# Strassen on a second level in the down products of an attention + SwiGLU kernel

## The chip, the cores and the metric

One core of a Trainium2 chip runs the whole kernel in one launch, in fp32. The metric is the device time of one execution in microseconds (us).

## What is computed

Cut to what matters, the reference is

```python
# transnormer attention: batch 8, heads 8, seq 576, head_dim 64
kv  = einsum('bhsd,bhse->bhde', k, v)          # 64x64 per head, over the sequence
o   = einsum('bhsd,bhde->bhse', q, kv)
x   = o / sqrt(mean(o*o, -1) + 1e-6) * g_norm  # -> (4608, 512): tokens x model
# SwiGLU: d_model 512, d_ff 1536
h   = silu(x @ w_gate) * (x @ w_val)           # the "up" stage
out = h @ w_out                                # the "down" stage, 4608 x 512
```

## The kernel before

The 4608 tokens are cut into 9 blocks of 512. The blocks run one after the other, and each has an **up** stage (gate and value products and their SwiGLU, class `Up` or `Inner`) and a **down** stage (class `Down`). Both stages save multiplications with Winograd's form of Strassen's algorithm: a product of 2x2 blocks is done by 7 products of blocks and some sums, with weight combinations made once and kept. The seven products are numbered 1 to 7 in the code, and `CHAIN` says which PSUM tile each adds to: 1, 6, 7, 4 run into one bank of tile `b`, 2 has tile `a`, 5 and 3 share one bank of tile `c`. PSUM has three buffers of `b`, two of `c`, one of `a` and two of `m`. A product that continues a bank must wait until the sum so far was read out of it.

From block 2 on (`DEEP = 2`) the up stage is Strassen on two levels: each of the outer 7 products is itself done by 7 products of 128x128 blocks (`Inner`). The weight blocks that this needs and that aren't kept in SBUF are prepared once, in block 1, and parked in DRAM. `Stream` loads them back in each later block, 51 DMAs of up to 256 KB, through a ring of nine `t` tiles. `Stream.pump` issues a load as soon as, in program order, the tile nine places back has been released.

The down stage of the kernel before is Strassen on one level. `Down.multiply` issues for each of its 7 products 12 matmuls of a 128x128 stationary block with 256 moving columns. Products 1, 6, 7 and 4 are copied out of PSUM by ScalarE (`after1`, `after6`, `after7`, `after4`), the others are added by VectorE. Three of the seven weight combinations are subtractions on GpSimd (`turn_t`), nine of them a block. VectorE makes the operand sums (`h_sums`, `turn_s3`, the one in `after2`).

While the down products run, the attention of the next block is done in between, by the closures of `Att.steps`: after product 1 `whole` (64 small matmuls, squares, root, scale, and the two 32x32 block transposes of `blocks_x`), after product 5 `place_x` (16 DMAs, 8 on the SP queue and 8 on ScalarE's, that put the transposed blocks of x in place), and after product 2 `end` (the gain on ScalarE, then the eight operand sums of x and xi on VectorE that the next up stage begins with).

The program is written down in that order, and a scheduler of the tile framework then moves instructions within it. What it leaves is a fixed order for each engine. The helper lambdas `add`, `sub` and `mul` are lines 111, 112 and 113, so most elementwise rows of the profile carry one of these three lines. `Inner`'s matmuls are line 728, `Quad`'s (so all of `Down`'s) line 565, the attention's lines 316 (k times v) and 361 (q times that).

Of the kernel before, what the change touches and what calls it, by code (L numbers as in the profile page):

```python
# [8 lines left out]
F32 = mybir.dt.float32  # L9
# [5 lines left out]
P = 128  # L15
# [3 lines left out]
def kernel(  # L19
# [41 lines left out]
    nc = tc.nc  # L61
# [4 lines left out]
    T = 4  # L66
    BLK = P * T
    HB = BLK // 2
    HD = DM // 2
# [3 lines left out]
    NP = NF // 2  # L73
# [12 lines left out]
    x_pool = pool("x", 1)  # L86
    h_pool = pool("h", 1)
    s_pool = pool("s", 1)
# [26 lines left out]
    def ring():  # L115

        return r_pool.tile([P, 4, BLK], F32, name="r")

    class Words:
# [12 lines left out]
        def __init__(self, src, shape):  # L132
            self.raw = ld_pool.tile([P, LD], U32, name="ld")[:, 0 : 2 * BLK]
            dst = self.raw.rearrange("p (a b) -> p a b", a=shape[0])
            self.sent = nc.sync.dma_start(out=dst, in_=src)
            self.shape = shape
            self.begun = False
# [55 lines left out]
    class Att:  # L193
# [308 lines left out]
        def steps(self):  # L502


            def whole():
                self.product(0, (m_psum, a_psum))
                self.product(1, (m_psum, b_psum))
                self.root(0, 2)
                for i in range(2):
                    self.scale(i)  # L510
                self.halves.append(self.scaled)
                self.blocks_x()

            def end():
                self.gain_x()
                self.sums()

            if self.n >= TURNED:
                return {1: whole, 5: self.place_x, 2: end}

            def last():
                self.turn_x(1)
                if self.n:
                    self.sums()

            def middle():
                self.turn_x(0)
                self.half(1, (m_psum, b_psum))


            return {1: lambda: self.half(0, (m_psum, a_psum)), 6: middle, 2: last}
# [128 lines left out]
    class Inner:  # L660
# [101 lines left out]
        def made3(self, p, e, q):  # L762
            if p != 4:
                return
            h = self.ffn.h[:, 4 * self.d : 4 * self.d + 4]
            c11, c12, c21, c22 = (self.whole(*i) for i in ((1, 1), (3, 1), (3, 0), (1, 0)))

            engine = nc.gpsimd if 4 * self.d + 4 < NF else nc.vector
            mul(engine, h[:, :, 0:HB], c11, c12)
            nc.scalar.activation(out=c21, in_=c21, func=ACT.Silu)  # L770
            mul(engine, h[:, :, HB:BLK], c21, c22)
            self.ffn.ended = self.ffn.h_sums(2 * self.d, 2, engine)


    RESIDENT = (1, 6, 2, 3)
# [8 lines left out]
        ((4, 5), (3, 5)), ((7, 4),), ((4, 2), (4, 3)), ((4, 7), (3, 7)), ((4, 4), (3, 4)),  # L784
    )

    class Stream:


        def __init__(self):  # L790
            self.dram = [dram.tile([P, len(LEAVES), 2, P], F32, name=f"w{d}") for d in range(NP // 2)]
            self.places = [sorted(map(LEAVES.index, ops)) for ops in CHUNKS]
            self.at = {LEAVES[i]: (c, m) for c, places in enumerate(self.places) for m, i in enumerate(places)}
            self.tiles, self.uses, self.next, self.held = {}, {}, [], []

        def enable(self, n):
            if DEEP <= n < NB:
                self.next += [(n, d, c) for d in range(NP // 2) for c in range(len(CHUNKS))]
                self.pump()

        def pump(self):

            while self.next and not self.held[-9]:
                n, d, c = key = self.next.pop(0)
                i, k = self.places[c][0], self.places[c][-1]
                count = len(CHUNKS[c])
                self.tiles[key] = t_tile(key).rearrange("p l (f c) -> p l f c", f=2)
                self.uses[key] = 2 * count
                nc.sync.dma_start(out=self.tiles[key][:, 0:count], in_=self.dram[d][:, i : k + 1 : max(k - i, 1)])

        def use(self, n, d, o, p, f):
            c, i = self.at[o, p]
            key = n, d, c
            self.uses[key] -= 1
            if not self.uses[key]:
                self.free(key)
            return self.tiles[key][:, i, f]

        def free(self, key):
            self.held = [None if k == key else k for k in self.held]  # L820
# [3 lines left out]
    def t_tile(key=None):  # L824

        stream.held.append(key)
        return t_pool.tile([P, 2, 2 * P], F32, name="t")
# [27 lines left out]
    class Down(Quad):  # L855
        def __init__(self, ffn):
            super().__init__(NP)
            self.ffn = ffn
            self.t = {}
            self.final = ffn.n == NB - 1  # L860
            if self.final:
                self.apart["c"] = None

        def turn_t(self, p, after=None):

            pairs = wo.rearrange("p (j e) d -> p e j d", e=2)
            of = {5: pairs[:, 1, :, HD:DM], 7: pairs[:, 0, :, 0:HD], 4: pairs[:, 1, :, 0:HD]}[p]
            self.t[p] = []
            for i in range(0, NP, 2):
                t = t_tile((self.ffn.n, p))  # L870
                turned = sub(nc.gpsimd, t, of[:, i : i + 2], pairs[:, 0, i : i + 2, HD:DM])
                if after:
                    tc.add_manual_dep(
                        turned.ins, after.ins.name,
                        mybir.DependencyInfo(mybir.DependencyClass.Sync, mybir.DependencyReason.DATA), reason="order",
                    )
                self.t[p] += [t[:, 0], t[:, 1]]

        def multiply(self, p):
            super().multiply(p)  # L880
            if p in self.t:
                stream.free((self.ffn.n, p))
            if p == 7:
                stream.enable(self.ffn.n + 1)
            stream.pump()

        def order(self, p):
            order = [(e, i) for e in range(2) for i in range(self.steps)]
# [45 lines left out]
        def add_c(self, o, u):  # L934
# [4 lines left out]
            for e, c in enumerate((self.ps["c"], self.apart["c"])):  # L939
                add(nc.vector, o[:, e], c[:, e], u[:, e])  # L940

    class Ffn:
        def __init__(self, n, att):
            self.n, self.att = n, att
# [9 lines left out]
        def h_sums(self, j, k, engine):  # L954
# [4 lines left out]
            add(engine, s1, a21, a22)  # L959
            return sub(engine, a21, s1, a11)  # L960

        def make(self, count):
            for _ in range(count):
                steps = self.making or self.later
                if steps:
                    steps.pop(0)()

        def up(self, fill):

            self.s1 = s_pool.tile([P, NP, HB], F32, name="s1")  # L970
            units = []
            for d in range(NP // 2):
                if self.n < DEEP:
                    units += [Up(self, 2 * d), Up(self, 2 * d + 1)]
                else:
                    shared = {}
                    units += [Inner(self, d, g, shared) for g in range(4)]
            units[0].prepare()
            last = None
            for i, this in enumerate(units):  # L980
                if i + 1 < len(units):
                    units[i + 1].prepare()
                for unit, p in this.sequence(last):
                    if unit:
                        unit.multiply(p)
                        self.make(4)
                last = this
                fill.get(12 * (i + 1) // len(units), lambda: None)()
            self.down_ = Down(self)
            self.down_.turn_t(5)  # L990
            for unit, p in last.sequence(None):
                if unit is None:
                    last.multiply(p)

        def down(self, nxt):

            down = self.down_
            fill = nxt.steps() if nxt else {}
            for p in (1, 6, 5, 7, 2, 4, 3) if 5 in fill else (1, 5, 6, 7, 2, 4, 3):
                if p == 1:  # L1000
                    down.turn_t(7, self.ended)
                if p == 6:
                    down.turn_t(4, nxt.halves[0] if nxt and nxt.n >= TURNED else None)

                with tc.issue_after(nxt.multiplied.ins) if self.n == 0 and p in (5, 6) else ExitStack():
                    down.multiply(p)
                self.make(12)
                if p in fill:
                    fill[p]()
                if p in (5, 7) and self.n == DEEP - 1:  # L1010

                    with tc.issue_after(nxt.scaled.ins), tc.issue_after(nxt.placed.ins):
                        room = self.leaf_room if p == 5 else ring().rearrange("p f (s c) -> p (f s) c", c=P)
                        for step in self.latest.pop(0)(room):
                            step()
                if p == 1:

                    with tc.issue_after(nxt.q_turned.ins) if self.n == 0 else ExitStack():
                        down.turn_s3()
# [152 lines left out]
```

## Time and profile before

| | us |
|---|---|
| median of 3 runs | 1023.45 |
| lowest and highest | 1023.36 and 1024.01 |
| span of the profiled execution, first to last instruction | 1021.4 |
| PE (TensorE matmul) busy in it | 1006.0 |
| DVE (VectorE) busy | 701.1 |
| POOL (GpSimd) busy | 369.0 |
| ACT (ScalarE) busy | 227.9 |

The profiled execution is listed with its span alone; the 2 us to the median of the runs lie before its first and after its last instruction. In the profile PE is the row of matmuls and PEld that of the weight loads which overlap them. An fp32 matmul leaves two PE records, so "x24" of a down product are its 12 matmuls. DVE is VectorE, ACT ScalarE, POOL GpSimd, SPq the queue of DMAs that SyncE issues. In a timeline line the columns are the start, the duration (of all merged instructions together), the engine, the line, the operation, the tiles, the count, and in brackets the idle time ahead of it with what ended it.

### The profile page before, as it was taken

The numbers are of one execution on the slowest core, as the hardware profiler recorded it, in microseconds if no ns is written. First come the engines' busy times: TensorE is split into PE (matmuls) and PEld (weight loads), VectorE is DVE, ScalarE is ACT, GpSimd is POOL, SyncE is SP. The second block draws the span as 40 slices with busy tenths as digits, with TensorE's granted clock in tenths as the row PEclk, the third lists the DMA queues.
The fourth block names the chain that finished last, engine by engine and source line by source line (L and its number), as shares of the span: only waits on it lengthen the run. The fifth ranks groups of instructions, "written<-read, shape, count | busy, mean of one in ns | idle before, by whom it ended". The sixth has DMA issues, their size and how long they took to land.

```text
span 1021.4 us, 21409 instructions
## 1 busy us (share of the span) xinstructions
PE 1006.0 (98%) x8522; PEld 897.1 (88%) x8522; DVE 701.1 (69%) x1169; ACT 227.9 (22%) x353; POOL 369.0 (36%) x280
## 2 busy tenths in 40 slices
PE   6999999999999999999999999999999999999998
PEld 4544688888999989998999899988998999989997
DVE  2999688998665946685558566665669466946661
ACT  2765112121211221121121211111121211221110
POOL 0000263534055503561246315630555045513670
PEclk9999999999999999999999999999999999999999
DMA  8689643767888377845686568636772766066601
GB/s 237 203 255 271 124 77 108 187 165 156 250 210 255 60 176 203 252 92 129 209 238 144 96 195 247 177 60 201 231 199 46 177 195 190 22 167 201 191 27 42
DMA packets 273845, 170.26 MB, mean 167 GB/s; under 512 B 150609, under 2 KB 241873, under 8 KB 273745
## 3 DMA queue, kind: packets, MB, share of 16 engines
q1 hardware_dynamic: 238800, 164.42, 59.3%
q10 hardware_dynamic: 34880, 4.46, 2.7%
q8 instruction: 68, 1.11, 0.4%
q14 instruction: 33, 0.26, 0.1%
q0 software_dynamic: 64, 0.00, 0.0%
HBM read 138.02 MB, written 22.41 MB: 157 GB/s over the span
## 4 chain that ended last, share of the span: by engine, by line
PE 90%; DVE 6%; DMA 2%; issue 1%; ACT 1%; SPq 0%; DVEq 0%; ACTq 0%
PE b L728 26%; PE b L565 19%; PE c L728 13%; PE c L565 10%; PE a L728 6%; PE a L565 5%; PE b L1032 4%; PE c L1032 4%; PE m L316 2%; PE m L361 1%; DVE r L112 1%; DVE xi L112 1%; DVE r L111 1%; DMA h<-in_v_dram 1%; DVE t L112 1%
## 5 line engine op out<-in xcount | busy, mean ns | idle before, releaser
L111 POOL TENSOR_TENSOR r<-r 128x256 f32<-128x256 f32 (+1 forms) x105 | 110.8, 1061 | 300.9 <-DVE r L111 272.2
L111 DVE TENSOR_TENSOR r<-b,r 128x512 f32<-128x512 f32 (+1 forms) x273 | 161.9, 606 | 65.5 <-PE b L728 60.1
L112 POOL TENSOR_TENSOR t<-wo 128x512 f32<-128x512 f32 x81 | 114.5, 1438 | 212.4 <-DVE wo L111 102.9
L111 DVE TENSOR_TENSOR r<-c,r 128x512 f32<-128x512 f32 (+1 forms) x179 | 108.5, 617 | 89.0 <-PE c L728 54.8
L728 PE MATMUL b<-x,t 128*128 128x128 f32 x1092 | 151.3, 276 | 0.0
L111 DVE TENSOR_TENSOR r<-a,r 128x512 f32<-128x512 f32 (+1 forms) x99 | 62.5, 631 | 113.4 <-PE a L565 70.7
L728 PEld LDWEIGHTS b<-x,t 128*128 128x128 f32 x1092 | 136.5, 192 | 0.8
L728 PE MATMUL c<-xi,t 128*128 128x128 f32 x840 | 112.4, 276 | 0.4 <-DVE xi L111 0.4
L113 POOL TENSOR_TENSOR h<-r 128x1024 f32<-128x1024 f32 (+1 forms) x40 | 82.3, 2072 | 76.9 <-DVE r L111 73.9
L728 PEld LDWEIGHTS c<-xi,t 128*128 128x128 f32 x840 | 102.9, 192 | 0.5 <-DVE xi L111 0.5
L565 PE MATMUL b<-wo,h 128*128 128x256 f32 x432 | 100.1, 383 | 0.1
L565 PE MATMUL b<-t,h 128*128 128x256 f32 x432 | 96.9, 381 | 0.0
L565 PEld LDWEIGHTS b<-t,h 128*128 128x128 f32 x432 | 81.6, 190 | 11.3 <-issue 0.2
L565 PEld LDWEIGHTS b<-wo,h 128*128 128x128 f32 x432 | 79.9, 190 | 13.1 <-DVE h L113 2.5
L742 ACT COPY r<-b 128x512 f32<-128x512 f32 x63 | 36.9, 585 | 211.6 <-PE b L728 211.6
L728 PE MATMUL b<-xi,t 128*128 128x128 f32 x588 | 79.8, 276 | 0.0
L728 PEld LDWEIGHTS b<-xi,t 128*128 128x128 f32 x588 | 72.4, 192 | 0.0
L728 PE MATMUL b<-x,wg 128*128 128x128 f32 x336 | 52.7, 279 | 0.2 <-DVE x L112 0.2
L728 PE MATMUL b<-x,wv 128*128 128x128 f32 x336 | 51.4, 276 | 0.0
L565 PE MATMUL a<-wo,h 128*128 128x256 f32 x216 | 48.3, 379 | 0.0
L565 PE MATMUL c<-t,s 128*128 128x256 f32 x216 | 48.1, 380 | 0.0
L565 PE MATMUL c<-wo,h 128*128 128x256 f32 x216 | 48.1, 379 | 0.0
(133 smaller groups left out, 1565.7 us busy)
## 6 DMA issues: line engine op xcount, KB each, us to landing
t<-w SPq DMA_DIRECT2D x336, 256.0 KB, 3.6
out_dram<-r SPq DMA_DIRECT2D x17, 512.0 KB, 3.1
ld<-in_k_dram SPq DMA_DIRECT2D x26, 288.0 KB, 5.2
ld<-in_v_dram SPq DMA_DIRECT2D x26, 288.0 KB, 5.9
ld<-in_moe_w_gate_dram SPq DMA_DIRECT2D x12, 512.0 KB, 4.8
ld<-in_moe_w_val_dram SPq DMA_DIRECT2D x12, 512.0 KB, 4.7
ld<-in_moe_w_out_dram SPq DMA_DIRECT2D x12, 512.0 KB, 4.9
w<-t SPq DMA_DIRECT2D x18, 256.0 KB, 3.0
```

The source lines that it names most:

```text
L111: add = lambda e, o, a, b: e.tensor_tensor(out=o, in0=a, in1=b, op=OP.add)
L112: sub = lambda e, o, a, b: e.tensor_tensor(out=o, in0=a, in1=b, op=OP.subtract)
L113: mul = lambda e, o, a, b: e.tensor_tensor(out=o, in0=a, in1=b, op=OP.mult)
L316: nc.tensor.matmul(self.kv_ps[r][u * D : (u + 1) * D, g, :], lhsT=k[:, u, c, :], rhs=v[:, u, c, :], start=(c == 0), stop=(c == KT - 1),)
L361: self.multiplied = nc.tensor.matmul(self.ps[i][u][p : p + D, t, j, :], lhsT=self.qt[rows, 2 * i + t, j, p : p + D], rhs=kvs[b % 3][rows, ...
L565: nc.tensor.matmul(banks[e][:, e], lhsT=lhsT, rhs=rhs, start=first and i == 0 and (e == 0 or banks[0] is not banks[1]), stop=i == self.ste ...
L728: nc.tensor.matmul(ps[:, i, f], lhsT=self.weight(o, p, f), rhs=self.operand(o, p), start=first and (i, f) == (0, 0), stop=True, skip_group ...
L742: nc.scalar.copy(out=dst, in_=ps)
L1032: nc.tensor.matmul(t, lhsT=w[f // 2][:, i, P * (f % 2) : P * (f % 2 + 1)], rhs=x[:, i, of], start=(i == 0), stop=(i == NS - 1),)
```

## The change

From block 3 on (`DEEPER = 3`) the down stage too is Strassen on two levels, in a new class `DeepDown`. The 7 outer products are taken in three groups, (1, 2, 4), (6, 5) and (3, 7), and each inner product of a group issues for each of its outer products 3 matmuls of 128x128 blocks with 128 moving columns. That makes 49 inner products of 3 matmuls. Each inner product of a group (7 a group, 21 in all) is taken out of PSUM into an `r` or `o` tile by one or two VectorE or ScalarE instructions; `row` then adds group results on GpSimd.

- **Weights.** For outer products 4, 5 and 7 all 7 inner weight blocks (of 3x128 columns each) come from DRAM: 21 loads a block. They are made once by `send_t` in the down stage of block 2, with GpSimd and 18 DMAs. For outer products 1, 2, 6 and 3 four come from the resident `wo`, which block 3's up stage turns in place with six GpSimd instructions, and three each, so 12 a block, are subtractions on GpSimd (`get_down`). Both kinds go through the nine `t` tiles.
- **Operands.** `turn_h` replaces `h_sums` and is two levels deep, on GpSimd for the first two thirds of h and on VectorE for the last. `go` makes the further ones: four leaf instructions and the outer sum s1 on VectorE, then two outer differences there, and nine leaf instructions on GpSimd. Two of these sets live in the `x` and `xi` tiles, which the next block's `place_x` and `end` fill afterwards.
- **The next block's attention** keeps its three closures; they now stand in `go` after product 5 of group 0, after product 7 of group 0 and after product 2 of group 1. Its first two PSUM tiles are `m` and `c` and no longer `m` and `a` when the block before is done by `DeepDown`.

```diff
             def whole():
-                self.product(0, (m_psum, a_psum))
+                self.product(0, (m_psum, c_psum if self.n > DEEPER else a_psum))
...
-            self.ffn.ended = self.ffn.h_sums(2 * self.d, 2, engine)
+            if self.ffn.n >= DEEPER:
+                self.ffn.turn_h(self.d, engine)
+            else:
+                self.ffn.ended = self.ffn.h_sums(2 * self.d, 2, engine)
...
+    DEEPER = 3
+    DOWN = (((1, 2, 4), (1, 5, 6, 3, 2, 7, 4)), ((6, 5), (1, 5, 6, 3, 2, 7, 4)), ((3, 7), (1, 5, 6, 3, 2, 7, 4)))
...
+        def get_down(self, to, o, p):
+            if o in RESIDENT:
+                e, g = PLACE[o]
+                m, c = {5: (1, 1), 7: (0, 0), 4: (1, 0)}[p]
+                sub(nc.gpsimd, to, wos[:, :, m, e, g, c], wos[:, :, 0, e, g, 1])
+            else:
+                nc.sync.dma_start(out=to, in_=self.down[o][:, DOWN_LEAVES.index(p)])
...
+    class DeepDown:
...
+        def multiply(self, group, p, ds=(0, 1, 2)):
+            outers = DOWN[group][0]
...
+            for i, o in enumerate(outers):
+                for d in ds:
+                    nc.tensor.matmul(
+                        ps[:, i], lhsT=self.operand(o, p, d), rhs=self.weight(o, p, d),
+                        start=first and (i, d) == (0, 0), stop=d == 2, skip_group_check=True,
+                    )
+            if ds[-1] == 2:
+                q, c = (self.ADDED if p in self.ADDED else self.MADE)[p]
+                dst = (self.r[:, 0:3], self.r[:, 0:4:3], self.o)[group][:, :, q, c]
+                if p in self.ADDED:
+                    add(nc.vector, dst, ps, dst)
+                elif group == 0:
+                    nc.scalar.copy(out=dst, in_=ps)
+                elif group == 1:
+                    add(nc.vector, dst[:, 0], ps[:, 0], dst[:, 0])
+                    nc.scalar.copy(out=dst[:, 1], in_=ps[:, 1])
+                else:
+                    add(nc.vector, dst, ps, self.r[:, 0:1, q, c].to_broadcast([P, 2, P]))
+            stream.pump()
...
+        def go(self, nxt):
...
+            self.multiply(0, 1, (0, 1))
+            self.multiply(0, 5, (0, 1))
+            fill[1]()
+            self.multiply(0, 1, (2,))
+            self.multiply(0, 5, (2,))
+            room = x_pool.tile([P, 7, 2, HB], F32, name="x").rearrange("p a b (c t) -> p (a b c) t", t=P)
+            for p in (3, 7):
...
+                self.leaf(
+                    vector, p, to[:, 0:2].rearrange("p o d t -> p d o t"), lambda m, q: h[:, :, m, :, 0, q]
+                )
+                self.leaf(vector, p, to[:, 2], lambda m, q: h[:, :, m, 1, 1, q])
...
+            self.multiply(0, 6)
+            self.s1 = s_pool.tile([P, NP, HB], F32, name="s1")
...
+            add(vector, self.s1, a21, a11)
...
+            for i, p in enumerate((5, 3, 7)):
+                for k, of in ((6, lambda m, q: h[:, :, m, 0, 1, q]), (5, lambda m, q: s1[:, :, m, q])):
...
+                    self.leaf(pool_, p, forms[k, p], of)
+            self.multiply(0, 3)
+            self.multiply(0, 2)
+            self.row(pool_, add, 1, r[:, 1], r[:, 0], 0)
+            self.multiply(0, 7)
+            fill[5]()
+            self.multiply(0, 4)
...
+            sub(vector, a11, a21, a22)
+            sub(vector, a12, a12, a21)
+            for p in (1, 5, 6, 3, 2):
+                self.multiply(1, p)
+            self.row(pool_, add, 0, r[:, 0], r[:, 3], 0)
+            fill[2]()
+            self.multiply(1, 7)
+            self.multiply(1, 4)
...
+            for p, to in ((5, h[:, :, 0, 1, 1]), (3, h[:, :, 0, 0, 1]), (7, h[:, :, 1, 1, 1])):
+                self.leaf(pool_, p, to, lambda m, q: h[:, :, m, :, 0, q])
...
+            for p in (1, 5, 6, 3, 2):
+                self.multiply(2, p)
...
+        def turn_h(self, d, engine):
...
+            add(engine, a21, a21, a22)
+            sub(engine, a21, a21, a11)
+            s2 = h[:, 0, :, :, 1]
+            add(engine, s2, s2, h[:, 1, :, :, 1])
+            sub(engine, s2, s2, h[:, 0, :, :, 0])
...
+            add(engine, to[:, 0:2], h[:, 0, :, 0, 1], h[:, 0, :, 0, 0])
+            return add(engine, to[:, 2], h[:, 0, 1, 1, 1], h[:, 0, 1, 1, 0])
...
+                if self.n == DEEPER - 1 and p in (5, 7, 4):
+                    down.send_t(p)
```

## The prediction

> **What bounds the kernel now.** I read the page's busy shares first, then the waits, then one down stage engine by engine.
>
> ```profile
> PE 1006.0 (98%) x8522; PEld 897.1 (88%) x8522; DVE 701.1 (69%) x1169; ACT 227.9 (22%) x353; POOL 369.0 (36%) x280
> ```
>
> PE never rests: the sum of matmuls is the time. So two things count: how many PE microseconds the change removes, and whether PE, which now waits for nobody, is made to wait. For that the down stage of block 6 is laid out, with zero at 773.7 us, where its last up product ends. PE:
>
> ```profile
> 773.64 4.34 PE L565 MATMUL b<-wo,h 128*128 128x256 f32 x18
> 779.94 5.45 PE L565 MATMUL b<-wo,h 128*128 128x256 f32 x24
> 785.22 5.34 PE L565 MATMUL c<-t,s 128*128 128x256 f32 x24
> 790.40 5.34 PE L565 MATMUL b<-t,h 128*128 128x256 f32 x24
> ...
> 811.12 0.61 PE L728 MATMUL b<-x,wg 128*128 128x128 f32 x4
> 811.57 0.61 PE L728 MATMUL b<-x,t 128*128 128x128 f32 x4
> ```
>
> Starts of equal groups are 5.18 us apart for 12 matmuls of 256 columns: 0.432 us each. The next up stage begins at 811.12, so the stage lasts 37.4 us. Groups of two 128-column matmuls start 0.447 us apart: 0.2235 each. VectorE in the same stretch:
>
> ```profile
> 774.71 2.36 DVE L113 TENSOR_TENSOR h<-r 128x1024 f32<-128x1024 f32 x2
> ...
> 780.30 2.46 DVE L375 TENSOR_REDUCE z<-r 128x8 f32<-128x512 f32 x4
> 782.80 1.22 DVE L381 TENSOR_SCALAR z<-z 128x32 f32<-128x32 f32 x1
> ...
> 788.77 2.36 DVE L420 STREAM_TRANSPOSE r<-r 128x1024 f32<-128x1024 f32 x2
> 800.97 0.69 DVE L111 TENSOR_TENSOR r<-a,r 128x512 f32<-128x512 f32 x1 [9.83 <-PE a L565]
> ```
>
> The reader is to see that the attention of the next block holds VectorE without a break from 774.7 to 791.1, that no down product needs VectorE in that time (ScalarE copies them), and that 9.83 us of rest follow. Last, the queues beside it:
>
> ```profile
> 791.19 7.19 SPq L434 DMA_DIRECT2D x<-r  x8
> 798.49 8.03 SPq L809 DMA_DIRECT2D t<-w  x7
> ```
> ```profile
> 778.66 5.32 POOL L112 TENSOR_TENSOR t<-wo 128x512 f32<-128x512 f32 x3 [6.71 <-DVE h L112]
> 788.93 3.72 POOL L112 TENSOR_TENSOR t<-wo 128x512 f32<-128x512 f32 x3 [4.95 <-DVE r L113]
> ```
>
> The placing of x holds SP for 7.2 us, and loads of weights queue behind it.
>
> [...] ScalarE's copy of product 7, whose matmuls end at 795.7, runs at 798.34, after its eight placing DMAs. [...] above, three subtractions take 1.77 us each beside VectorE's sums and 1.24 each beside its scaling and transposes. [...]
>
> **The change part by part.**
>
> *Matmuls.* Removed 84 x 0.432 = 36.3 us a block, added 147 x 0.2235 = 32.9. Gain 3.4 us in each of blocks 3 to 8, 20.5 in all, if nothing waits.
>
> *VectorE.* Gone from a down stage: three PSUM adds (2.1), two differences (3.5), h sums (1.4), 7.0 us. Added: six instructions of `turn_h` (four of 512 elements, one of 256, one of 128: 3.5), four leaves (2 x 0.96 + 2 x 0.56 = 3.0), s1 and two differences (3 x 1.76 = 5.3), and PSUM reads: 3 x 0.56 in group 0, 4 x 0.29 + 3 x 0.42 in group 1, 7 x 0.42 in group 2, together 7.0. Net +11.8 us; the queue holds about 27 us in these 37 now, then 39. In sum that nearly fits the 34.9 us (147 matmuls and the attention's 2.0) plus the slack of the up stage (47.0 busy of 67). The order doesn't fit. In the built program VectorE's first read of PSUM by this stage, product 2 of group 0 from tile `a`, stands behind the h products (2.36, from 1.0), `turn_h` (3.5), squares (2.46), leaves (3.0), s1 (1.76), root (3.6), scale (2.4) and transposes (2.36): 1.0 + 21.4 = 22.4, done at 23.0. Tile `a` has one buffer, and PE's queue reaches the next `a` product (group 1, product 2) after 48 matmuls from zero (10.7), the attention (2.0) and 2.6 us in which product 5 waits for the last of `turn_h`: 15.4. **First stall: 15.4 to 23.1.**
>
> *GpSimd.* Its queue holds, behind that read, a `row` (0.74), weights (1,4) and (2,4), and only then (6,5), which group 1's product 5 needs. At 1.1 us for 384 elements (between 1.24 and 1.77, times three quarters): 23.5 + 0.7 + 3.3 = 27.6. PE, at 24.9 after three matmuls and 36 small ones of the next attention (1.1), stalls 2.8.
>
> *Placing x.* Behind those three matmuls PE ends product 7 of group 0, at 29.0. `place_x` writes the `x` tile that this product reads, so it starts at 29.2 instead of 17.5 and lands at 36.4; with the gain (2.2) x is ready at 38.7. Behind it on SP wait the loads (5,7), (5,4), (7,1): the third lands at about 41 (3.6 us each by the page). Behind it on ScalarE wait two copies of group 1.
>
> *Differences.* VectorE reads product 7 (29.8), then product 1 of group 1 (32.8), then makes the two differences: 36.3. PE's next matmul, group 2's product 1, needs the second: at 33.6 it stalls to 36.4. GpSimd's leaves of h follow: 2 x 2.0, `row` 0.8, (6,4) 1.1, 2.0, then (3,5) 1.1: 45.3. PE, which waited 1.2 us for (7,1), is there at 42.9 and stalls 2.4. From 45.3, 42 matmuls and three of the next up stage (10.1): 55.5.
>
> So the stage takes 55.5 instead of 37.4, of which 1.1 are small matmuls of a later stage: **+17.0 us in each of blocks 3 to 7, 85 us.**
>
> *The rest.* Block 8 has no attention behind it: 3.4 gained, some 5 lost at its start and in the GpSimd chain: +2 (-3 to +6). In block 2, `place_x` stands on SP behind six of `send_t`'s DMAs, whose last GpSimd step comes at about 24 instead of 17.5: +5 (0 to +10). GpSimd's deeper `turn_h` in the up stage, 2 x 3.7 us more on 33.8 of 67, and block 3's six turns of `wo` (8 us) hide in its rest: 0 to +1 a block, I take 0. The 21 loads are 4.1 MB, some 118 GB/s beside 125 in this stretch, under the page's 271: 0. Slower GpSimd beside a fuller VectorE: 0 to +3 a block; half clock after the 7.7 us stall: 0 to +2 a block, since later waits are not PE's own; I take 0 for both. ScalarE has eight smaller copies for four (about 2.9 us for 2.3) on 8.35 busy of 38: 0, its rest hides them. The stores of the result wait on GpSimd's last `row` and hold SP, but nine loads, some 11 us of up matmuls, stand ahead of them: 0.
>
> Sum on the profiled execution: 1021.4 + 85 + 2 + 5 = 1113.4; the median stands 2.0 above that span: **1115**.
>
> **The rivals.**
> - *VectorE's first read alone counts*, and the GpSimd, SP and difference waits hide behind it. From 23.1 PE has 93 matmuls (20.8) and 1.1 us left: 45.0, so +6.5 a block, and 1023.4 + 32 = 1056. For it: the longest stall is certain from the order, the others hang on estimates of 1 us. Against: each stands in the queue order by itself.
> - *Faster.* The operand work fits into VectorE's 9.83 us of rest, PE loses nothing and the 20.5 us come, less the 5 of the entry: 1008. It decides at one point: VectorE's read of `a` must be done by 15.4. It would need 7.6 of the 21.4 us ahead of it gone; these are durations from rows, so little speaks for it.
> - *Slower still.* GpSimd at 1.77 us and half clock: +5 a block, 1140.
> - That the matmuls are not the fewer: the built order has 49 x 3 of 128 columns a stage. Excluded.
>
> **How the numbers follow.** Walk as worked out 0.54, VectorE alone 0.26, slower still 0.12, faster 0.06, and 0.02 for a middle that cancels to no change. Under 0.2% (2 us) a measurement of this kernel can't tell from none. Range 1055 to 1140: from the second case to the third.
>
> **What would show it.** In the profile after: four PE records of the new matmuls 0.447 us apart where nothing waits; in each down stage from block 3 to 7 a PE wait on VectorE's read of `a` of about 7 us and further ones of 2 to 3 on GpSimd and on `h`; `place_x` 26 to 30 us after the stage's start; a stage near 55 us and no rest on VectorE before 22 us. It is wrong if PE stays at 97% or more, or if the read of `a` comes before 15.4.

## The result and the profile after

The changed kernel takes 1128.7 us (1127.1 to 1131.5 in 4 runs), 1.1028 times the kernel before (95% interval 1.1011 to 1.1044). The profiled execution has a span of 1125.3 us against 1021.4. The page of the changed kernel, its first busy row and the granted clock in 40 slices:

```profile
PE 1028.1 (91%) x9278; PEld 934.1 (83%) x9278; DVE 800.6 (71%) x1307; ACT 230.2 (20%) x377; POOL 551.7 (49%) x482
...
PEclk9999999999999999989997999989998999889999
```

The 103.9 us of span are 82 us more of PE waiting (97.2 idle against 15.4) and 22 us more of PE *busy*, though the matmuls should have become 20.5 us shorter. The clock row has 9 in all slices before, and now 7 and 8 in some: part of the matmuls ran at a lower clock (0.969 on average, 1.000 before). What PE waits for (tile it wants, whose instruction ended the wait; us in total, times, longest):

```profile
PE a L1048 <- DVE r L111: 19.4, 3, 7.4
PE c L1048 <- DVE s L111: 15.7, 12, 2.8
PE b L1048 <- ACT r L1061: 10.3, 10, 2.1
PE b L1048 <- DVE s L111: 9.8, 3, 5.5
```

Before, PE waited for nobody in a down stage. The three waits of the first line are those of blocks 3, 4 and 5 (7.4, 6.1 and 5.9 us). Blocks 6 and 7 have none: the scheduler left PE another order there. PE waits 5.5 and 4.2 us for the outer sum s1 (almost all of the last line), and the next `a` product comes so late that nothing is left to wait for, though VectorE's read of `a` ends no earlier (25.7 and 26.9 us after the last up product, 24.1 to 25.6 in blocks 3 to 5). Block 6:

```profile
852.62 1.22 PE L1048 MATMUL b<-t,s 128*128 128x128 f32 x4 [5.50 <-DVE s L111]
...
865.28 0.83 PE L1048 MATMUL a<-wo,h 128*128 128x128 f32 x6
```

From the first up product of one block to that of the next, in us:

| block | 3 | 4 | 5 | 6 | 7 | 8 (to the end) |
|---|---|---|---|---|---|---|
| before | 107.8 | 107.8 | 107.7 | 108.4 | 104.5 | 105.8 |
| after | 132.9 | 128.7 | 125.7 | 121.9 | 123.1 | 114.5 |
| more | 25.1 | 21.0 | 18.0 | 13.5 | 18.5 | 8.8 |

Now the down stage of block 4, laid out as the prediction laid out that of block 6, with zero at 581.4. It has the wait for `a`, and it is the longest of the five (58.7 us; the others last 51.9 to 56.6). PE's timeline (start, us, instruction, count of records, idle ahead with its releaser):

```profile
581.38 1.50 PE L1048 MATMUL c<-t,s 128*128 128x128 f32 x12
...
590.09 0.79 PE L1048 MATMUL c<-t,s 128*128 128x128 f32 x4 [2.75 <-DVE s L111]
...
597.93 1.50 PE L1048 MATMUL b<-t,x 128*128 128x128 f32 x12
605.56 1.65 PE L1048 MATMUL a<-wo,h 128*128 128x128 f32 x6 [6.12 <-DVE r L111]
609.69 1.65 PE L1048 MATMUL c<-t,xi 128*128 128x128 f32 x6 [0.78 <-POOL t L112]
611.67 1.65 PE L1048 MATMUL b<-t,x 128*128 128x128 f32 x6
...
624.48 0.94 PE L1048 MATMUL c<-wo,xi 128*128 128x128 f32 x6 [1.47 <-ACT r L1061]
...
640.10 0.61 PE L728 MATMUL b<-x,wg 128*128 128x128 f32 x4
```

Six records are three matmuls. Where nothing waits, such groups start 0.67 us apart, 0.2235 each as foreseen; after the wait for `a` the same six take 1.65, twice the time. VectorE beside it:

```profile
602.71 2.36 DVE L420 STREAM_TRANSPOSE r<-r 128x1024 f32<-128x1024 f32 x2
604.99 0.52 DVE L111 TENSOR_TENSOR r<-a,r 128x384 f32<-128x384 f32 x1
...
613.36 0.56 DVE L111 TENSOR_TENSOR r<-b,r 128x384 f32<-128x384 f32 x1 [7.39 <-PE b L1048]
615.99 3.43 DVE L112 TENSOR_TENSOR h<-h 128x1536 f32<-128x1536 f32 x2 [2.08 <-PE b L1048]
```

The read of `a` follows the transposes without a gap: VectorE's queue sets it. After it and one read of `c`, VectorE is idle for 7.39 us, waiting for the PE that waited for it. ScalarE, with the placing of x that it shares with SP:

```profile
613.40 7.21 ACTq L434 DMA_DIRECT2D x<-r  x8
620.71 0.48 ACT L1058 COPY r<-b 128x384 f32<-128x384 f32 x1 [24.10 <-DMA x<-r]
...
624.16 0.27 ACT L1061 COPY r<-c 128x128 f32<-128x128 f32 x1 [2.81 <-DVE r L111]
624.48 2.19 ACT L441 ACTIVATE x<-x,gain 128x1024 f32<-128x1024 f32 x2
```

The gain of x stands behind a copy that waits for a read on VectorE, which in turn waited 1.97 us for GpSimd's `row`. That is how the three queues pass a delay on, here one of 1 us: the last part of x landed at about 623.5. The stage as a whole, busy time of each engine in the stretch from zero to the next up product, with the mean granted clock and DMA's share and GB/s behind:

```profile
581.40:640.10 58.70, 44.27 (x472) 40.88 (x471) 40.87 (x60) 7.97 (x15) 26.63 (x24) 0.85 0.55 124
```

PE idles 14.4 us of 58.7 and is busy 44.3 at a mean clock of 0.85; the prediction had 19.5 idle and 36.0 busy. The stage length is nearly the same (55.5 and 58.7), its make-up isn't.

### The profile page after: what moved, and what is told of

Its sections match the earlier page's. It is cut to its first block, busy times and chain, and to the rows that moved or that the text cites. A ratio compares the mean times of both kernels' runs of the same rounds, so it can differ in the third digit from the quotient of the medians.

```text
span 1125.3 us, 23659 instructions
## 1 busy us (share of the span) xinstructions
PE 1028.1 (91%) x9278; PEld 934.1 (83%) x9278; DVE 800.6 (71%) x1307; ACT 230.2 (20%) x377; POOL 551.7 (49%) x482
## 4 chain that ended last, share of the span: by engine, by line
PE 69%; DVE 15%; DMA 5%; issue 4%; POOL 3%; ACT 2%; ACTq 2%; SPq 0%; POOLq 0%; DVEq 0%
PE b L728 23%; PE c L728 12%; PE b L565 7%; PE a L728 6%; PE b L1048 4%; PE c L565 4%; PE b L1284 4%; PE c L1284 4%; DVE x L112 2%; DVE xi L112 2%; PE a L565 2%; DVE r L111 2%; DVE s L111 2%; ACTq L434 2%; DMA x<-r 2%
## 5 line engine op out<-in xcount | busy, mean ns | idle before, releaser
L111 DVE TENSOR_TENSOR r<-b,r 128x512 f32<-128x512 f32 (+3 forms) x327 | 182.5, 569 | 106.7 <-PE b L728 60.9
L111 POOL TENSOR_TENSOR r<-r 128x256 f32<-128x256 f32 (+1 forms) x139 | 140.5, 1023 | 207.7 <-DVE r L111 177.2
L112 POOL TENSOR_TENSOR t<-wo 128x384 f32<-128x384 f32 (+1 forms) x99 | 117.5, 1203 | 163.6 <-DVE wo L111 102.9
L111 DVE TENSOR_TENSOR r<-c,r 128x512 f32<-128x512 f32 (+2 forms) x195 | 112.6, 586 | 74.1 <-PE c L728 52.8
L111 DVE TENSOR_TENSOR r<-a,r 128x512 f32<-128x512 f32 (+2 forms) x111 | 66.4, 598 | 76.8 <-PE a L728 44.3
L1048 PE MATMUL b<-t,h 128*128 128x128 f32 x432 | 62.7, 290 | 7.9 <-DVE r L111 6.6
L1048 PE MATMUL b<-wo,h 128*128 128x128 f32 x288 | 47.3, 314 | 9.5 <-ACT r L1061 8.2
L112 POOL TENSOR_TENSOR h<-h 128x512 f32<-128x512 f32 (+1 forms) x36 | 52.3, 1453 | 1.9
L111 POOL TENSOR_TENSOR h<-h 128x512 f32<-128x512 f32 (+1 forms) x30 | 41.4, 1379 | 22.8 <-DVE h L112 20.9
L1048 PEld LDWEIGHTS b<-wo,h 128*128 128x128 f32 x288 | 42.2, 224 | 12.0 <-ACT r L1061 9.3
L112 DVE TENSOR_TENSOR h<-h 128x1536 f32<-128x1536 f32 (+1 forms) x30 | 41.2, 1390 | 8.8 <-PE b L1048 6.6
```

Of the source, the lines that this page charges most:

```text
L111: add = lambda e, o, a, b: e.tensor_tensor(out=o, in0=a, in1=b, op=OP.add)
L112: sub = lambda e, o, a, b: e.tensor_tensor(out=o, in0=a, in1=b, op=OP.subtract)
L1048: nc.tensor.matmul(ps[:, i], lhsT=self.operand(o, p, d), rhs=self.weight(o, p, d), start=first and (i, d) == (0, 0), stop=d == 2, skip_gro ...
```

## The experiments

The prediction's walk is a chain of waits, and its first rival puts all on VectorE's read of `a`. The expectations below split this into three theories. **Queue theory**: the next block's attention, which VectorE does ahead of the stage's first PSUM reads, makes most of the loss. **Chain theory**: GpSimd's weights and the placing of x set the length of the stage anyway. **Matmul theory**: the small products with their streamed weights are slow by themselves. "The chain" in the headings and tables below is the attention's reduces, root and scale on VectorE. Two further questions came up: the clock, and whether the placing of x sets the end.

### One block, two blocks

```diff
-    DEEPER = 3
+    DEEPER = 8      # first run: block 8 alone; second run: 7, blocks 7 and 8
```

Block 8 alone. 

> The two-level down stage in block 8 alone (DEEPER = 8), which has no attention of a next block behind it. From the trace of the changed kernel block 8 alone takes 8.8 us more and the entry (the preparing of the weights a block earlier) nothing: 1032. Queue theory (the next block's attention on VectorE ahead of the stage's first PSUM reads makes most of the loss): block 8 costs far less than the 19 us of a block with attention, 1024 to 1033. Matmul theory (the small products with their streamed weights are slow by themselves): as much as any other block, 1040 or more.

Blocks 7 and 8. 

> The two-level down stage in blocks 7 and 8 (DEEPER = 7): one block with attention behind it more than in the run with block 8 alone. Queue theory: +13 to +20 us over that run, with one PE wait of 5 to 7 us on VectorE's read of tile a. Matmul theory: the same step as from none to block 8, 9 us.

Measured: 1037.8 us, ratio 1.0130 (1.0115 to 1.0145), and 1055.2 us, ratio 1.0301 (1.0285 to 1.0316). The first block that has an attention beside it costs 17.4 us, the prediction's step was 17.0. The entry (the preparing of the weights one block earlier) and block 8 cost 13.0 together, where the prediction had 7 and the expectation 9: the number lies above the range of the queue theory and below that of the matmul theory. The stretch from block 8's first up product to the end, before and then in the first kernel:

```profile
915.65:1021.40 105.75, 102.43 (x757) 97.54 (x755) 53.45 (x85) 15.71 (x22) 42.65 (x32) 1.00 0.39 117
...
921.69:1036.20 114.51, 102.62 (x883) 99.82 (x881) 75.91 (x111) 16.28 (x26) 78.13 (x62) 1.00 0.56 169
```

So even with no attention and no lost clock to be seen, PE's busy time doesn't fall, and it idles 11.9 us for 3.3. The waits are 0.2 to 1.4 us each and 7.7 together: 4.2 for reads of PSUM on ScalarE and VectorE, 1.3 for a sum of x in the up stage, the rest for sums and leaves of h. What idle time remains lies after the last matmul.

### The attention's chain taken out

```diff
-                self.root(0, 2)
+                if self.n <= 3:
+                    self.root(0, 2)
...
+                if self.n > 3:   # scale(): ScalarE instead of VectorE
+                    self.scaled = nc.scalar.copy(out=self.xts[:, i, :, :, u], in_=self.ps[i][u])
+                    continue
```

The reduces go in the same way. In the changed kernel: 

> The changed kernel, but from block 4 on the squares are not summed, the root is left out and x is not scaled: ScalarE copies the attention's products to where VectorE's scaling would have put them. This takes 8.5 us (2.46 + 3.6 + 2.4) off VectorE ahead of the first PSUM read of the five down stages with attention, and leaves the transposes. Queue theory: the read of a comes by 15 us, the long PE wait is gone, and a block gains 8 to 12 us: 1068 to 1090. Chain theory (GpSimd's weights and the placing of x set the stage anyway): under 4 us a block, above 1108.

The same edit in the kernel before, as a control: 

> The kernel before with the same parts of the attention left out from block 4 on, as a control. Both theories: VectorE had 9.8 us of rest here and PE no wait, so the same time within 3 us, 1020 to 1025; the read of x by the next up stage can come a little earlier and changes nothing.

Measured: 1091.3 us, ratio 1.0656 (1.0629 to 1.0684), and 1023.3, ratio 0.9986 (0.9979 to 0.9993). Before, the chain was hidden within 2 us; after, it costs 37.4 us, 7.5 a block on average (4.9 to 9.7 from the end of one down stage to the end of the next, and nothing in block 8), just under the queue theory's 8 to 12. The wait for `a` is gone in every block: in block 4 the read comes 16.8 us after zero instead of 23.6, and it waits for PE now. Nearly two thirds of the loss stay, so neither the wait for `a` nor the chain is all of it. VectorE's other work ahead of the read (`turn_h`, leaves, s1, transposes) was left in, so this says nothing of the rest of its queue.

### The read of `a` met in two other ways

In the first kernel PE's order is changed: product 2 of group 1, the one that needs `a`, comes after the whole of group 0's product 7, to fill the wait.

```diff
+                    with tc.issue_after(self.seventh.ins) if (group, p) == (1, 2) else ExitStack():
                         nc.tensor.matmul(
```

> The changed kernel with one ordering edge: on PE, product 2 of group 1 stands behind the whole of product 7 of group 0, where the scheduler had put it ahead of that product's last three matmuls. Nothing else is asked for. Queue theory, in its fuller form (the wait for tile a also holds back product 7, and with it place_x and VectorE's next reads): place_x starts some 23 us after the last up product instead of 32, a block with attention gains 3 to 7 us, 1094 to 1113. If only the lateness of VectorE counts, PE waits as long for the read of product 7 instead: under 2 us a block, above 1118.

In the second, VectorE's order: root, scale and transposes are written down after product 7, so that the reads stand ahead of them.

```diff
             self.multiply(0, 7)
+            fill['rest']()      # root, scale, transposes of the next attention
             fill[5]()
```

> The changed kernel with the attention's root, scale and transposes written down after product 7 of group 0 instead of after product 5, so that VectorE's reads of tiles c and a stand ahead of them; all work is done. Queue theory: the read of a comes by 15 us after the last up product, and a block gains 6 to 12 us: 1068 to 1098. Chain theory: x is placed no earlier, so the stage ends as late as now: above 1118.

Measured: 1132.3 us, ratio 1.1056 (1.1039 to 1.1072), and 1127.7, ratio 1.1008 (1.0992 to 1.1025). The changed kernel has 1.1028 (1.1011 to 1.1044), so neither gained anything, where the queue theory had gains of 16 to 61 us; the interval of the first lies slightly higher, but the two overlap. In both the wait for `a` is gone from PE's list. In the first, PE's block 4 (zero near 583.7) has in its place

```profile
611.98 1.65 PE L1049 MATMUL c<-t,xi 128*128 128x128 f32 x6 [6.08 <-POOL t L112]
```

a wait for GpSimd's weight (6,5), that is of outer product 6, inner product 5. GpSimd makes it after a `row` that waits for VectorE's read, so it comes when it came before, and the matmul that needs it still stands ahead of the rest of product 7. In the second (zero near 582.5) VectorE reads early, and the chain comes late:

```profile
598.86 0.56 DVE L111 TENSOR_TENSOR r<-a,r 128x384 f32<-128x384 f32 x1 [0.49 <-PE a L1052]
...
607.69 2.36 DVE L420 STREAM_TRANSPOSE r<-r 128x1024 f32<-128x1024 f32 x2
...
613.94 4.23 DVE L112 TENSOR_TENSOR h<-h 128x1536 f32<-128x1536 f32 x2 [1.50 <-PE b L1052]
```

The read is at 16.4 after zero, the transposes end at 27.5 (23.7 in the changed kernel), the differences at 35.7 (38.0). PE has a new wait in the same stage, for the tile `m` that VectorE's scale hasn't read yet:

```profile
606.03 3.38 PE L316 MATMUL m<-ld 64*64 64x64 f32 x72 [4.53 <-DVE r L113]
```

So the wait for `a` is where PE meets the lateness, not its cause: taken away, it comes back at GpSimd's weight or at `m`. Blocks 6 and 7, which never had it, say the same: they still cost 13.5 and 18.5 us.

### GpSimd's weights taken out

```diff
-            if o in RESIDENT and p in QUARTER:
+            if o in RESIDENT:
                 e, g = PLACE[o]
-                m, c = QUARTER[p]
+                m, c = QUARTER[p if p in QUARTER else {5: 1, 7: 6, 4: 2}[p]]
```

> After with GpSimd's subtractions of weights left out: products 5, 7 and 4 of the four outer products with resident weights use blocks that lie there already, so their part of the output is another one. The attention chain, the loads and the sums on VectorE stay. Walk of the prediction: GpSimd's two waits a block (2.8 us for the weight of product 5 of group 1, 2.4 us for that of group 2) go, in blocks 3 to 8 some 5 us each: 1128.7 - 31 = about 1098. Rival, the attention chain and the sums of x behind it set the end of the stage, and GpSimd's waits only stand ahead of it: 1122 to 1129. In between, one of the two waits was on the path.

Measured: 1094.2 us, ratio 1.0702 (1.0671 to 1.0732), 34.5 below the changed kernel: the walk's number was 1098. Counted in the same way, block 4 gains 10.5 us and each of the other five 4.8 to 5.7, block 8 without an attention included; the walk had some 5 a block. PE's list of waits no longer has `a`. Yet VectorE reads `a` as late as ever: block 4's zero is 574.5 there, and

```profile
598.60 0.54 DVE L111 TENSOR_TENSOR r<-a,r 128x384 f32<-128x384 f32 x1
```

is 24.1 us after it (23.6 in the changed kernel). What changed is PE's order. Without weights to wait for, the program has product 7 of group 0 and more of group 1 ahead of the next `a` product:

```profile
600.84 1.60 PE L1048 MATMUL b<-wo,h 128*128 128x128 f32 x12 [1.80 <-DVE r L111]
...
602.96 0.61 PE L1048 MATMUL c<-t,xi 128*128 128x128 f32 x4
603.40 0.83 PE L1048 MATMUL a<-wo,h 128*128 128x128 f32 x6
...
619.33 0.61 PE L728 MATMUL b<-x,wg 128*128 128x128 f32 x4
```

The `a` product runs at 28.9 after zero with no wait. The next up stage begins at 44.8 (58.7), but that overstates the gain: 21 matmuls of the down stage stand behind that point here, 6 in the changed kernel, and the last of them ends at 53.8 (61.0). This run takes GpSimd's time out, moves the order with it and lets 12 of a block's 33 down weights skip the ring of `t` tiles; the share of each isn't separated. That blocks 3 and 5, which lose a wait for `a`, gain no more than blocks 6 and 7, which had none, speaks for GpSimd's time.

### Both taken out, and the placing too

Chain and weights: 

> No GpSimd weight subtractions, and from block 4 on also no reduces, root and scale of the attention on VectorE (ScalarE copies stand in for the scale). If chain and GpSimd's weights are two losses that add up: 1091.3 (chain left out alone) - 25 to 31 = 1060 to 1066. If the weights cost only as long as the chain delays them: 1085 to 1091. If they cost only once the chain is gone: as the first number, with no gain in the kernel that has the chain.

These two, and the 16 placing DMAs replaced by a ScalarE copy:

```diff
+            if self.n > 3:
+                self.placed = nc.scalar.copy(
+                    out=self.x[:, 0:4].rearrange("p o k t -> p (o k t)"), in_=self.turned.rearrange("p i x -> p (i x)")
+                )
+                return
```

> No weight subtractions, no reduces, root and scale from block 4 on, and the 16 placing DMAs replaced by one ScalarE copy (x of the later blocks is not the reference's). What stays is the 147 matmuls a stage, the h sums, the leaves, the reads of PSUM and the sums behind them on VectorE and ScalarE. If the waits that the prediction named are the whole loss, the matmuls' gain of 3.4 us a block shows from block 4 on: 1023.7 - 17 + about 25 for block 3, which keeps its chain = 1030. If the many short waits for sums and reads within a group are a loss of their own, as in block 8 of the kernel that is changed there alone (some 9 us a block): 1060 to 1090.

The placing alone, chain and weights kept: 

> The changed kernel, but x is moved to its place by one ScalarE copy (about 2 us) instead of 16 DMAs from block 4 on, so its blocks stand in the wrong order. SP is free of the 7.2 us of placing, and the loads behind it. Chain theory: 5 us a block or more, below 1103. Queue theory: the long wait for tile a stays, and what is gained behind it is under 4 us a block, 1108 to 1128.

| left out | us | ratio (interval) | against the changed kernel |
|---|---|---|---|
| chain | 1091.3 | 1.0656 (1.0629 to 1.0684) | -37.4 |
| weights | 1094.2 | 1.0702 (1.0671 to 1.0732) | -34.5 |
| both | 1060.3 | 1.0358 (1.0342 to 1.0373) | -68.4 |
| both and placing | 1057.8 | 1.0330 (1.0314 to 1.0345) | -70.9 |
| placing alone | 1134.1 | 1.1074 (1.1056 to 1.1093) | +5.4 |

Chain and weights add up (37.4 + 34.5 = 71.9 against 68.4): two losses, not one behind the other. The runs were taken on several chips; reckoned by the ratios, the five differences move by 1.1 us at most. Each holds the clock's part too: PE's mean clock is 0.969 in the changed kernel, 0.982 without the chain, 0.980 without the weights and 0.992 without both. The placing by DMA is no loss that these runs show, though both theories had that kernel no slower than the changed one. The copy in its place holds ScalarE for 1.9 us. With x in place earlier, VectorE takes the sums of x earlier, beside GpSimd, and the reads of PSUM queue behind them. VectorE in that kernel, block 4:

```profile
624.85 4.17 DVE L112 TENSOR_TENSOR x<-x 128x512 f32<-128x512 f32 x2
628.94 0.28 DVE L111 TENSOR_TENSOR r<-b,r 128x128 f32<-128x128 f32 x1
```

Two sums that take 1.81 us in the changed kernel take 4.17, and PE waits 3.50 us for a copy on ScalarE that comes after the read behind them. With chain and weights out, 36 us above before remain, of which only a part is traced. In block 4 of that kernel PE's waits are 2.3 us for the sums `s` of h, 1.8 and 0.8 for weights from DRAM, 0.9 for GpSimd's leaf and 0.4 for a read: 6.3, together more than the 3.4 that the matmuls save.

### The clock

26 more matmuls into a bank's unused quarter after product 7 of group 0, with the changed PE order, meant to keep PE busy in the wait.

```diff
+                    for _ in range(26):
+                        with tc.issue_after(last.ins):
+                            last = nc.tensor.matmul(
+                                self.ps[name][:, 3], lhsT=self.operand(1, 1, 0), rhs=self.weight(1, 1, 0),
+                                start=False, stop=True, skip_group_check=True,
+                            )
```

> The same edge, and 26 extra matmuls of 128x128 blocks (5.8 us at full clock) behind product 7 of group 0 into an unused quarter of its bank, in the five stages with attention: they lie in the wait for VectorE and only keep PE busy. Clock theory (half clock after the long wait costs 2 to 4 us a block): 10 to 20 us less than the run with the edge alone. If the clock costs nothing because later waits hide it: the same, or up to 10 us more where the extra matmuls outlast the wait.

Measured: 1155.2 us, ratio 1.1268 (1.1249 to 1.1288), 23 us more than with the changed order alone. In block 4 the fill began after product 7, and so after a wait of 5.15 us for GpSimd's weight, too late to keep PE busy in it. Its 26 matmuls took 7.57 us there (5.8 at 0.2235 each), and the mean clock fell from 0.966 to 0.961. The run shows that PE has no room for more matmuls there; what the clock costs it doesn't settle.

## Why the prediction was right

**The walk.** Block 4, in us after zero:

| step | predicted | measured |
|---|---|---|
| wait of product 5 for `turn_h` | 2.6 | 2.75 |
| PE reaches the next `a` product | 15.4 | 18.0 |
| VectorE's read of `a` done | 23.0 | 24.1 |
| stall on it | 7.7 | 6.1 |
| product 5 of group 1, after GpSimd's weight | 27.7 | 28.3 |
| `place_x` starts | 29.2 | 32.0 |
| x has its gain | 38.7 | 45.3 |
| second difference done | 36.4 | 38.0 |
| weight (3,5) ready | 45.3 | 46.0 |
| next up stage | 55.5 | 58.7 |

So the queue orders and the sizes from rows (0.54 us for a PSUM read of 384, 0.96 foreseen, 1.15 and 0.94 measured for the two leaves of 768, 1.00 for GpSimd's 384 where 1.1 was taken) carried the walk to 3 us of its end. For sizes with no row the prediction's 0.56 and 0.96 are estimates: a straight line through VectorE's PSUM reads of 256 and 512 elements in the trace before (417 ns in 84 instructions, 690 in 189, tile `b`) gives 0.55 for 384 and 0.96 for 768. From zero to the next up product the five stages became 14.4 to 20.3 us longer, 87.2 together, where 85 were predicted. Blocks 3 to 7 as a whole cost 96.0; most of the rest is block 3's up stage, 6.9 longer, where the entry shows.

**What was luck.** The times of the walk came true, its waits only in part. Of its six stalls, 19.5 us in sum, the first two came (3.0 and 6.1 in block 4, for 2.6 and 7.7). Of the other four, 9.2 in sum (GpSimd's two weights, the second difference, a load from DRAM), 0.8 was left, because PE itself was late by then. In their place PE waited 4.4 us for copies and reads of PSUM that the walk didn't have, and was busy 8.3 us longer. And the wait for `a`, foreseen in all five blocks, is in three. The total, 1128.7, lies a little nearer to the case *slower still* (1140) than to the walk (1115).

**Readings that were off** in the trace before, without changing the walk: of the stretch given to the attention, 774.7 to 791.1, the first 5.6 us are h's own products and sums, which the down products do need. The three subtractions of 1.77 us each took 2.87, 1.27 and 1.27, so that only the first was slow beside a VectorE sum. And the stretch has 107 GB/s and 7.7 us of ScalarE, for 125 and 8.35.

**Matmuls.** The price of 0.2235 us held, the gain of 20.5 us didn't show anywhere. It was counted on a PE that works without a break at full clock. PE's busy time lies 42.6 us above that count (22.1 more where 20.5 less was foreseen). Part of it comes with the breaks themselves: six records take 0.94 after a wait and 0.83 without. The larger part, by the estimate below, is the clock.

**Half clock.** Taken as 0, with 0 to 2 a block kept for the range: the author's guess, for the trace before shows no lowered clock. In the changed kernel block 4's stage has two stretches at a granted clock of 0.50, 17 us in all; the longer one is the first line below. There are 13 of them up to the last matmul, 68 us, and the second line is their sum:

```profile
604.20:617.85 13.65, 11.51 (x106) 10.41 (x107) 4.19 (x6) 0.00 (x0) 4.58 (x5) 0.50 0.27 48
sum 68.05, PE 54.30 PEld 51.80 DVE 45.29 ACT 6.77 POOL 33.52; mean PE 4.18 PEld 3.98 DVE 3.48 ACT 0.52 POOL 2.58
```

PE was busy for 54.3 us of these. As the groups above take twice their time there (1.65 us for 0.83), some 27 us of busy time are due to the clock; this is an estimate from these lines. In the wait of 6.12 us, from 599.44 to 605.56, the granted clock is 1.00 up to 604.2 and 0.50 from there to 617.9. After the wait of 2.75, which ends at 590.09, it is 1.00 up to 590.6 and 0.50 to 594.0, and the nine matmuls from 592.54 took 2.88 us, where 2.17 follow from the 0.67 and 0.83 of an undisturbed group. What sets the clock these runs don't show. By an estimate from the same lines the stretch of 3.4 us at 0.50 took 1.7 of the 2.6 us by which PE came to `a` later than predicted, and the stall then was shorter: half speed within a stage that waits anyway costs less than its own time. How much is left isn't known.

**x with its gain** is the step that was off most, 6.6 us. 2.8 of them are the later start. Nearly 3 are a misreading: 7.2 us is the time in which the 16 DMAs are *issued*, and each lands 2.5 to 4.7 us after its issue, so x was there 10.1 us after the start. The kernel before had it too, with the placing from 791.19 and the gain at

```profile
801.40 2.19 ACT L441 ACTIVATE x<-x,gain 128x1024 f32<-128x1024 f32 x2 [2.48 <-DMA t<-w]
```

The last 1.0 us is the copy ahead of the gain on ScalarE, which waits for VectorE and GpSimd. All this cost little, because PE's last products don't need x and VectorE's sums of x and xi end at 638.2, ahead of the up stage at 640.1.

**Block 8** was put at +2 (-3 to +6) and measured +8.8: the mis-sized term is the some 5 us of its start and its GpSimd chain, which left out the short waits between groups that the kernel with block 8 alone shows.

**The entry**, +5 (0 to 10), was 4.2 in the kernel with block 8 alone (13.0 less 8.8) and 6.9 in the changed kernel's block 3. In the changed kernel `place_x` of block 2 moved from 358.5 to 364.3, 5.8 us, as predicted from `send_t`. Then the sums of xi ran beside the six turns of `wo` on GpSimd, which had been put at 0; VectorE at the start of block 3:

```profile
383.79 2.11 DVE L111 TENSOR_TENSOR xi<-x 128x896 f32<-128x896 f32 x1
385.82 2.15 DVE L112 TENSOR_TENSOR xi<-x 128x896 f32<-128x896 f32 x1
```

They take 1.09 each before, where GpSimd was idle; here its turns of `wo` run beside them, from 381.9 to 389.1. The sums end 10 us later than before, PE waits 2.9 us in five short waits for them and for a PSUM read behind them.

**The rivals.** *VectorE alone* (1056) falls: with the chain out 67 us of the loss are left, and moving the read gained nothing. *Faster* (1008) falls with the read at 24.1. *Slower still* (1140) named slow subtractions on GpSimd and half clock; the subtractions took 1.00 us, less than the 1.1 of the walk, and half clock came, 0.50 in 68 us.

What the prediction had wrong in kind is that it took the stall on `a` as the first cause and the GpSimd wait as what follows. The runs show it the other way as well: without GpSimd's weights the order has no such stall, and in two of the five blocks it had none at all.

## What to carry to other kernels

Fewer multiplications pay only as far as the engines that make the operands and empty PSUM have room at the moment when PE needs them (here 20.5 us were to be saved, and PE waited 82 us more); where PE never waited, follow each other queue in order and add up what stands ahead of the first instruction that PE needs. A wait that is the longest in the list isn't a cause yet: take away what stands behind it, and see whether the wait moves or the time does. Two losses are told apart by leaving out each alone and both. And one block is not all blocks: here the scheduler left other orders, and other waits, in blocks that do the same work.

## What the runs showed of the hardware

VectorE's 32-element steps of the root take 0.17 to 0.19 us, and 0.65 to 1.22 in the cases below, where a GpSimd instruction runs beside them. With the root written down later, the step at 599.34 took 1.02 us and ended 0.04 after GpSimd's two subtractions at 598.37 to 600.32, and the next took 0.65 and ended 0.04 after GpSimd's addition (600.27 to 601.00). Each ended with the end of a GpSimd instruction that ran beside it; why is not shown. The prediction's own lines have such a step, 1.22 us at 782.80 beside a GpSimd subtraction. In block 4's stage of the changed kernel three such steps cost 2.8 us of the chain in place of 0.6.
